# Spare PSUM banks for attention in block 0, later weight splits and loads, and global queries turned without a copy

## The chip, the cores and the metric

The kernel runs on one core of one Trainium2 chip. The metric is device time in microseconds. The kernel before took 1093.67 us, the median of three runs (1090.04 to 1094.86). The profile shown is of one further execution.

## The reference

Sliding-window attention with a few global tokens is followed by a gated MLP, all in f32. Batch 8, 8 heads, 512 local tokens, 32 global tokens, head size 64.

```python
s_g = scale * q_g @ k_all.T          # global queries see all 544 keys
out_g = softmax(s_g) @ v_all
s_ll = where(|i - j| <= 32, scale * q_l @ k_l.T, -1e9)
s_lg = scale * q_l @ k_g.T           # local queries see 65 neighbours and the 32 global keys
out_l = softmax([s_lg, s_ll]) @ [v_g, v_l]
x = [out_g, out_l] as (8 * 544, 512) rows
h = x @ w_in                          # 512 -> 2048
y = (h * sigmoid(h)) @ w_out          # 2048 -> 512
```

## The kernel before, in words

**Tiles and blocks.** The 4352 rows of x are 34 tiles of 128 tokens. A tile of local tokens (batch b, chunk c) is made by four attention steps, one for each pair of heads (pr); k counts the steps, 128 in all. Two further tiles hold the global queries' rows. The MLP takes the tiles in blocks (SIZES, L38): block 0 has one tile, blocks 1 to 11 have three each. A block's MLP has 16 steps f, one for each 128 columns of d_ff: `first_layer(n, f)` (L599) makes h, applies the gate on ACT and DVE, and `second_layer(n, f)` (L628), one step behind, adds to the block's outputs.

**Numbers.** The precision needed is kept in two ways. Early work (attention steps k < 28 for the scores and k < 16 for the rest, batches b < 3 for the global heads, block 0's MLP) is computed in plain f32. Later operands are split into a high and a low part in fp32r, and products are the sum of two or three matmuls. So the weights are wanted in f32 for block 0 and as w_hi and w_lo from block 1 on. They come as 8-byte words: `fetch_weights` (L167) loads a half slice (512 KB) by a DMA that ACT issues, `join_weights` (L175) makes f32 of it with one operation on ACT (L193) and two on DVE (L195, L196), and `split_weights(f)` (L199) makes w_hi on ACT (L206) and w_lo on POOL (L207) for each half of a slice. All of these are pinned behind what was written before them for their engine. The f32 slice 15 lives in the two buffers of klo, which the attention steps from k = 28 on use for the low part of k.

**One attention step.** `st_load`, `st_vload` (DMAs from SP), `st_split`, `st_vsplit`, `st_scores` (PE scores into a bank "s", DVE mask and maximum at L361, ACT exponentials at L365, scaling), `st_turn` (the probabilities are transposed on PE into a bank "t" and copied to pt by ACT, the global columns added by POOL), `st_out` (PE into a bank "o", emptied by ACT and DVE, L459 to L464 or L470 to L471).

**Global heads.** For each batch, `g_load`, `g_split`, `g_scores` (PE into banks "s" and "o", copied to pg by ACT) and `g_soft` run beside the batch before. `g_move` (L266), for b >= 3, copies the 128 x 512 part of pg to an fp32r tile rg with a DMA from SP; rg takes a buffer "o" of the pool `two`, whose two buffers also hold the finished output rows (L645). `g_turn` (L274) transposes four pieces on PE into a bank "o" (gt, L291; from pg in f32 for b < 3, from rg in fp32r for b >= 3), and the last 32 columns into a bank "s" (gu, L294); ACT and DVE copy them out (L292, L297, L298).

**PSUM.** There are eight banks: one each for "s", "t" and "o" (`attbank`, L75), two for h, three for the block's outputs (out0 to out2). Before block 0's MLP begins ("early"), attention also rotates through h and out banks; `early.clear()` ends that. Block 0 has one tile and uses out0 alone.

**The order of the work.** PE executes in the order of the program. The attention steps form a list sorted by due times (`put`, the tables DUE, LATE, HEAD, TURN, MOVE); `fill` (L585) is called after each piece of the MLP and issues from this list so that block n + 1's attention is written out while block n's MLP runs. The other engines' order is made by a scheduler from the program. FIRSTW and FIRSTC say at which early attention steps how many weight halves are fetched and joined; in block 0, step f joins up to slice f + 1 and fetches up to slice f + 3 (LOOK, FETCH). Slice i is split at MLP step SPLIT0 + i, counted from block 0's first step (L663). At a block's last step the program issues from the list until no rg waits for its turn (L642).

Of the kernel before, what the change touches and what calls it, by code (L numbers as in the profile page):

```python
# [9 lines left out]
F32 = mybir.dt.float32  # L10
F32R = mybir.dt.float32r
# [9 lines left out]
P = 128  # L21
# [20 lines left out]
GF = 3  # L42
KP = 12
SCRATCH = 8
FETCH, LOOK = 4, 2
SPLIT0, SPLITS = 11, 1.0
FIRSTW = {1: 2, 2: 1, 3: 1}
FIRSTC = {2: 1, 3: 1}
LATE = dict(load=-1.0, first=0.2, head=0.8, soft=0.3, turn=1.0, slot=4.0)

DUE = dict(load=-1.2, split=-0.5, vload=-0.6, vsplit=0.95, turn=1.6, out=2.2)
LAG = 2.25
HEAD = dict(load=-0.2, split=0.45, scores=0.65, soft=0.85, slot=0.3)
HEADS0, HEADS = (10, 1), (7, 2)
MOVE, TURN = (-0.3, -0.8), (0.7, 1.7)
FULL = 0.98
END = 0.5

# [1 line left out]
def attention_moe_kernel(ctx: ExitStack, tc: tile.TileContext, qk0_in, qk_in, v_in, gqk, wts, out):  # L60
    nc = tc.nc
# [4 lines left out]
    two = ctx.enter_context(tc.tile_pool(name="two", bufs=2))  # L66
# [3 lines left out]
    ps_out = ctx.enter_context(tc.tile_pool(name="ps_out", bufs=1, space=PSUM))  # L70


    early, banks = [1], {"s": itertools.count(), "t": itertools.count(), "o": itertools.count()}

    def attbank(kind, name):  # L75
        if early:
            i = next(banks[kind]) % {"s": 3, "t": 2, "o": 3}[kind]
            if i and kind == "s":
                return ps_h.tile([P, 512], F32, tag="h", name=name)
            if i:  # L80
                return ps_out.tile([P, 512], F32, tag="out2" if kind == "t" else f"out{i - 1}", name=name)
        return ps_att.tile([P, 512], F32, tag=f"att{kind}", name=name)


# [2 lines left out]
    ident = const.tile([P, P], F32R, name="ident")  # L87
# [31 lines left out]
    pgs = [const.tile([P, SKV], F32, name=f"pg{i}") for i in range(2)]  # L119
# [90 lines left out]
    state = {}  # L210
# [39 lines left out]
    def did(what, *needs):  # L250
        for need in needs:
            assert need in order_done, (what, need)
        order_done.add(what)
# [9 lines left out]
        nc.vector.reciprocal(out=st[:, 3:4], in_=st[:, 0:1])  # L263
        nc.vector.tensor_scalar(out=pg, in0=pg, scalar1=st[:, 3:4], scalar2=None, op0=ALU.mult)

    def g_move(b, hh):  # L266
        did(("move", b, hh), ("soft", b, hh))
        if b < GF:
            return
        r0 = two.tile([P, 4 * P], F32R, tag="o", name=f"rg0_{b}_{hh}")  # L270
        nc.sync.dma_start(out=r0.bitcast(F32), in_=pgs[hh][:, : 4 * P])
        state["rg", hh] = r0

    def g_turn(b, hh):  # L274
        whole = b < GF
        if whole:
            r0, idt = pgs[hh], ident.bitcast(F32)
        else:
            r0, idt = state.pop(("rg", hh)), ident
        did(("turn", b, hh), ("turn", b, 0) if hh else ("last", b - 1))  # L280
        if hh == 0:

            state["pgt"] = (work.tile([P, NC, H, SG], F32, tag="pgt", name=f"pgt{b}"),
                            work.tile([P, QG], F32R, tag="pgh", name=f"pgh{b}"),
                            work.tile([P, QG], F32R, tag="pgl", name=f"pgl{b}"))
        pgt, pgh, pgl = state["pgt"]
        hs = slice(4 * hh, 4 * hh + 4)
        tb = attbank("o", f"gt{b}_{hh}")
        for i in range(4):
            sl = slice(i * P, (i + 1) * P)  # L290
            nc.tensor.transpose(tb[:, sl] if whole else tb[:, sl].bitcast(F32R), r0[:, sl], idt)  # L291
        nc.scalar.copy(out=pgt[:, :, hs, :], in_=tb.rearrange("p (t h q) -> p t h q", t=4, h=4))  # L292
        tb = attbank("s", f"gu{b}_{hh}")
        nc.tensor.transpose(tb[:SG, :P], pgs[hh][:, 4 * P :], ident.bitcast(F32))  # L294
        for i in range(2):
            rows, src = slice(SG * (2 * hh + i), SG * (2 * hh + i + 1)), tb[:SG, QG * i : QG * (i + 1)]
            nc.scalar.copy(out=pgh[rows, :], in_=src)  # L297
            nc.vector.tensor_tensor(out=pgl[rows, :], in0=src, in1=pgh[rows, :].bitcast(F32), op=ALU.subtract)  # L298
# [219 lines left out]
    stream, marks = [], {}  # L518
    at = 0.0

    def put(when, fn, *a):
        stream.append((when, fn, a))

    AHEAD = NPR * SIZES[0]
    for k, (t, b, c, pr) in enumerate(steps):
        a = (k, b, c, pr)
        j = k % NST
        lag = LAG if k < AHEAD else 0.0
        if k == AHEAD:
            at += LAG + LATE["first"]  # L530
            for h in range(NPR):
                due = at + LATE["head"] * h
                put(due + LATE["load"], g_load, 0, h)
                put(due, g_scores, 0, h)
                if h % 2:
                    put(due + LATE["soft"], g_soft, 0, h // 2)
                    put(due + LATE["soft"], g_move, 0, h // 2)
                    put(due + LATE["soft"] + LATE["turn"], g_turn, 0, h // 2)
            at += LATE["slot"]
            put(at + DUE["turn"] - 0.1, g_late)  # L540
        if j == 0 and b:
            for hh in range(2):
                put(at + MOVE[hh], g_move, b, hh)
                put(at + TURN[hh], g_turn, b, hh)
        for counts, fn in ((FIRSTW, fetch_weights), (FIRSTC, join_weights)):
            for i in range(counts.get(k, 0)):
                put(at + DUE["load"], fn)
        put(at + DUE["load"], st_load, *a)
        put(at + DUE["split"], st_split, *a)
        put(at, st_scores, *a)  # L550
        put(at + lag + DUE["vload"], st_vload, *a)
        put(at + lag + DUE["vsplit"], st_vsplit, *a)
        put(at + lag + DUE["turn"], st_turn, *a)
        put(at + lag + DUE["out"], st_out, *a, t)
        marks[t] = at + lag + DUE["out"]
        if j == NST - 1 and b % 4 == 3:
            put(marks[t] + 0.001, g_tile, t + 1)
            marks[t + 1] = marks[t] + 0.001
        if b + 1 < B:
            for h in [h for h in range(NPR) if int((HEADS if b else HEADS0)[0] + h * (HEADS if b else HEADS0)[1]) == j]:  # L560
                for part, fn in (("load", g_load), ("split", g_split), ("scores", g_scores)):
                    put(at + HEAD[part], fn, b + 1, h)
                if h % 2:
                    put(at + HEAD["soft"], g_soft, b + 1, h // 2)
                at += HEAD["slot"]
        at += 1.0
    stream.sort(key=lambda e: e[0])
    done = 0

    def advance(to):  # L570
        nonlocal done
        while done < len(stream) and stream[done][0] <= to:
            _, fn, a = stream[done]
            done += 1
            fn(*a)

    ends, t = [], 0
# [50 lines left out]
    def second_layer(n, f, gh, gl):  # L628
        if f == 0:
            outs[n] = [ps_out.tile([P, DM], F32, tag=f"out{i}", name=f"out{n}_{i}") for i in range(SIZES[n])]  # L630
        wh, wl = (w_hi[f][:, DM:], w_lo[f][:, DM:]) if n else (w_32[2 * f + 1], None)
        for i, o in enumerate(outs[n]):
            sl = slice(i * P, (i + 1) * P)
            if n == 0:
                nc.tensor.matmul(o, gh[:, sl], wh, start=(f == 0), stop=(f == NF - 1))
            else:
                nc.tensor.matmul(o, gh[:, sl], wh, start=(f == 0), stop=False)  # L637
                nc.tensor.matmul(o, gh[:, sl], wl, start=False, stop=False)  # L638
                nc.tensor.matmul(o, gl[:, sl], wh, start=False, stop=(f == NF - 1))  # L639
            fill(1)  # L640
        if f == NF - 1:
            while ("rg", 0) in state or ("rg", 1) in state:  # L642
                advance(stream[done][0])
            for i, o in enumerate(outs.pop(n)):
                sb = two.tile([P, DM], F32, tag="o", name=f"o{n}_{i}")  # L645
                nc.scalar.activation(sb, o, AF.Copy, scale=0.5)
                for p0, np_, r in out_rows(sum(SIZES[:n]) + i):
                    nc.sync.dma_start(out=out[r : r + np_, :], in_=sb[p0 : p0 + np_, :])
# [4 lines left out]
    for n in range(len(SIZES)):  # L653
        for f in range(NF):
            if n == 0:
                while w_next[1] < 2 * min(NF, f + LOOK):
                    join_weights()
                while w_next[0] < 2 * min(NF, f + FETCH):
                    fetch_weights()
            elif f == 0:  # L660
                advance(ends[n])
                now[:] = n, 0
            while len(w_hi) < NF and SPLIT0 + SPLITS * len(w_hi) <= NF * n + f:  # L663
                split_weights(len(w_hi))
            g = first_layer(n, f)
            fill(SIZES[n])
            if pend is not None:
                second_layer(*pend)
            pend = (n, f, *g)
# [70 lines left out]
```

## Time and profile before

| | |
|---|---|
| median of three runs | 1093.67 us (1090.04 to 1094.86) |
| the profiled execution | 1088.63 us, span 1086.8 us, granted clock 0.991 |
| PE busy | 1033.7 us, 95% |
| DVE busy | 749.4 us, 69% |
| ACT busy | 734.9 us, 68% |
| POOL busy | 189.6 us, 17% |
| block 0's MLP | from 24 us to 126 us |
| block 1's MLP | from 126 us to 223 us |
| bytes moved by DMA | 128.63 MB |

PE is TensorE, DVE is VectorE, ACT is ScalarE, POOL is GpSimd, SP is SyncE; PEld is the load of weights into TensorE, which overlaps its matmuls. L206 is line 206 of the kernel. Groups of instructions are shown as `line engine operation out<-in shape xcount | busy us, mean ns | idle before <-releaser`; lines in order of time as `start us, length us, engine line operation out<-in`, with the idle time before and its releaser in brackets; waits as `engine line <- what it waited for: us in total, times, longest`. "issue" is waiting for nothing that the profile shows.

### The profile page before, as it was taken

Reading aid. Unit: us, or ns where it says so; the run is one execution under the profiler, and the core shown is the slowest. Engines: PE = TensorE matmul, PEld = TensorE weight load, DVE = VectorE, ACT = ScalarE, POOL = GpSimd, SP = SyncE. Lnnn points to the kernel's source line nnn. Section 1 sums busy time; section 2 is a strip of 40 time slices with the busy share of each in tenths; the row PEclk is TensorE's granted clock in tenths of the full one; section 3 lists DMA queues with packets and bytes.
Section 4 is the critical chain, followed back from the end, with each engine's and each line's share of the span. In section 5 each row is a group of like instructions: output and inputs, shape, how many; then the busy total and the mean of one; then the engine's idle time right before and its main releaser. Section 6 shows DMA issues by size and latency. Waiting matters only on the chain.

```text
span 1086.8 us, 19886 instructions
## 1 busy us (share of the span) xinstructions
PE 1033.7 (95%) x6168; PEld 926.3 (85%) x6168; DVE 749.4 (69%) x2285; ACT 734.9 (68%) x1977; POOL 189.6 (17%) x480
## 2 busy tenths in 40 slices
PE   5786798999999999999999999999999999999997
PEld 4564697899999899999999988998999989999996
DVE  3778574677778777886657877778777877654322
ACT  5676676777778677776657777777777877654322
POOL 2004475211111111111101111111111211110000
PEclk9998999999999999999999999999999999999999
DMA  7885132343344334343224434434433533410000
GB/s 242 283 283 177 63 98 86 113 132 104 111 139 129 122 110 141 124 140 114 72 78 127 155 98 130 123 118 130 140 112 119 161 100 113 127 40 21 30 1 29
DMA packets 68745, 128.63 MB, mean 118 GB/s; under 512 B 7712, under 2 KB 27680, under 8 KB 68640
## 3 DMA queue, kind: packets, MB, share of 16 engines
q1 hardware_dynamic: 64032, 110.59, 32.3%
q10 hardware_dynamic: 4608, 16.78, 4.5%
q8 instruction: 49, 0.80, 0.3%
q14 instruction: 56, 0.46, 0.1%
HBM read 86.44 MB, written 8.91 MB: 88 GB/s over the span
## 4 chain that ended last, share of the span: by engine, by line
PE 87%; DVE 4%; ACT 4%; issue 2%; DMA 1%; POOL 0%; ACTq 0%; DVEq 0%; POOLq 0%
PE h L612 33%; PE out L637 12%; PE out L639 11%; PE out L638 11%; PE s L357 5%; PE o L448 4%; PE o L450 3%; PE t L392 3%; DVE w L196 1%; PE o L444 1%; PE gs L240 1%; ACT probs L365 1%; DMA raw<-in_qk_dram 1%; ACT w_hi L206 1%; PE gt L291 1%
## 5 line engine op out<-in xcount | busy, mean ns | idle before, releaser
L612 PE MATMUL h<-xh,w_hi 128*128 128x384 f32 x704 | 241.4, 343 | 0.0
L612 PE MATMUL h<-xl,w_hi 128*128 128x384 f32 x704 | 238.3, 339 | 0.0
L612 PE MATMUL h<-xh,w_lo 128*128 128x384 f32 x704 | 238.3, 339 | 0.0
L637 PE MATMUL out<-w_hi,gh 128*128 128x512 f32 x528 | 219.6, 416 | 0.0
L639 PE MATMUL out<-w_hi,gl 128*128 128x512 f32 x528 | 208.8, 395 | 0.3 <-DVE gl L625 0.3
L638 PE MATMUL out<-w_lo,gh 128*128 128x512 f32 x528 | 208.1, 394 | 0.0
L618 ACT ACTIVATE t<-h 128x384 f32<-128x384 f32 (+1 forms) x192 | 90.6, 472 | 158.9 <-PE h L612 152.1
L620 DVE SCALAR_TENSOR_TENSOR t<-t,h 128x384 f32<-128x384 f32 x176 | 97.2, 552 | 113.1 <-ACT t L618 111.8
L612 PEld LDWEIGHTS h<-xh,w_hi 128*128 128x128 f32 x704 | 133.0, 189 | 5.1
L612 PEld LDWEIGHTS h<-xl,w_hi 128*128 128x128 f32 x704 | 132.9, 189 | 5.1
L612 PEld LDWEIGHTS h<-xh,w_lo 128*128 128x128 f32 x704 | 132.6, 188 | 0.0
L625 DVE TENSOR_TENSOR gl<-t,gh 128x384 fp32r<-128x384 f32 x176 | 99.2, 563 | 46.1 <-PE out L639 40.4
L365 ACT ACTIVATE probs<-probs,st 128x224 f32<-128x224 f32 x244 | 115.7, 476 | 12.1 <-DVE st L361 10.7
L416 POOL CAST pt_hi<-pgt 128x64 fp32r<-128x64 f32 x112 | 37.7, 336 | 490.1 <-PE o L450 347.7
L639 PEld LDWEIGHTS out<-w_hi,gl 128*128 128x128 f32 x528 | 99.5, 188 | 23.8 <-DVE gl L625 0.7
L361 DVE CUSTOM_DVE_ANT_0 probs<-s,mask 128x224 f32<-128x224 f32 x244 | 85.2, 385 | 43.7 <-PE s L357 42.7
L637 PEld LDWEIGHTS out<-w_hi,gh 128*128 128x128 f32 x528 | 100.0, 189 | 12.4 <-issue 2.0
L638 PEld LDWEIGHTS out<-w_lo,gh 128*128 128x128 f32 x528 | 100.3, 190 | 10.5
L624 ACT CAST gh<-t 128x384 fp32r<-128x384 f32 x176 | 89.8, 510 | 21.5 <-DVE t L620 18.8
L471 DVE TENSOR_TENSOR xs<-o,xs 64x160 f32<-64x160 f32 x224 | 70.7, 315 | 28.5 <-ACT xs L470 24.3
L327 ACT CAST qk<-raw 128x704 fp32r<-128x704 f32 x100 | 78.1, 781 | 16.3 <-PE s L357 14.9
L448 PE MATMUL o<-pt_hi,vv 128*128 128x160 f32 x448 | 87.7, 264 | 0.6 <-DVE xs L471 0.3
(122 smaller groups left out, 1871.8 us busy)
## 6 DMA issues: line engine op xcount, KB each, us to landing
raw<-in_qk_dram SPq DMA_DIRECT2D x100, 352.0 KB, 3.0
rr<-probs SPq DMA_DIRECT2D x112, 256.0 KB, 2.3
raw_w<-in_wts_dram ACTq DMA_DIRECT2D x32, 512.0 KB, 5.7
vraw<-in_v_dram SPq DMA_DIRECT2D x128, 128.0 KB, 2.3
raw_g<-in_gqk_dram SPq DMA_DIRECT2D x32, 304.0 KB, 2.9
out_dram<-o SPq DMA_DIRECT2D x32, 256.0 KB, 2.6
raw<-in_qk_dram SPq DMA_DIRECT2D x28, 240.0 KB, 4.4
rg<-pg SPq DMA_DIRECT2D x10, 256.0 KB, 2.8
```

What stands on the lines that cost most here:

```text
L327: nc.scalar.copy(out=qk, in_=raw)
L361: nc.vector.tensor_tensor_reduce(out=p[:, u, :W], in0=s[:, u * W : (u + 1) * W], in1=mask_of[c], scale=-SCALE, scalar=3.0e38, op0=ALU.add, ...
L365: nc.scalar.activation(p[:, u, :W], p[:, u, :W], AF.Exp, bias=st[:, u : u + 1], scale=-1.0, accum_out=st[:, 2 + u : 3 + u])
L448: nc.tensor.matmul(o[:, at], vv[:, a, u].rearrange("p t d -> p (t d)"), pt_hi[:, u, a, :m], start=(a == 0), stop=(a == 1))
L612: nc.tensor.matmul(h[:, :nt], wt, x[:, c, :nt], start=(i == 0), stop=(i == 3 * NCC - 1))
L618: nc.scalar.activation(t[:, :nt], h[:, :nt], AF.Tanh, scale=0.5)
L620: nc.vector.scalar_tensor_tensor(out=out[:, :nt], in0=t[:, :nt], scalar=1.0, in1=h[:, :nt], op0=ALU.add, op1=ALU.mult)
L624: nc.scalar.copy(out=gh[:, :nt], in_=t[:, :nt])
L625: nc.vector.tensor_tensor(out=gl[:, :nt], in0=t[:, :nt], in1=gh[:, :nt].bitcast(F32), op=ALU.subtract)
L637: nc.tensor.matmul(o, gh[:, sl], wh, start=(f == 0), stop=False)
L638: nc.tensor.matmul(o, gh[:, sl], wl, start=False, stop=False)
L639: nc.tensor.matmul(o, gl[:, sl], wh, start=False, stop=(f == NF - 1))
```

## The change

Four things change.

- In `attbank`, once "early" is over and until block 1's first step, every second tile of the kind "s" takes the bank out1 and every second tile of the kind "o" takes out2 (the list `spare` is cleared at block 1's first step).
- SPLIT0 goes from 11 to 14: slice i is split at MLP step 14 + i, so slices 0 and 1 in block 0 and the other fourteen in block 1.
- FIRSTW goes from {1: 2, 2: 1, 3: 1} to {0: 2, 1: 1, 2: 1, 3: 2}, and these fetches and the two joins of FIRSTC are due just behind the scores of their step rather than with its load, 1.2 units earlier.
- `g_move` is gone, with the loop that waited for rg at a block's end: `g_turn` transposes pg itself, in f32, for all batches.

```diff
-SPLIT0, SPLITS = 11, 1.0
-FIRSTW = {1: 2, 2: 1, 3: 1}
+SPLIT0, SPLITS = 14, 1.0
+FIRSTW = {0: 2, 1: 1, 2: 1, 3: 2}
...
-MOVE, TURN = (-0.3, -0.8), (0.7, 1.7)
+TURN = (0.7, 1.7)
...
-    early, banks = [1], {"s": itertools.count(), "t": itertools.count(), "o": itertools.count()}
+    early, spare, banks = [1], [1], {"s": itertools.count(), "t": itertools.count(), "o": itertools.count()}
...
+        elif spare and kind != "t" and next(banks[kind]) % 2:
+            return ps_out.tile([P, 512], F32, tag="out1" if kind == "s" else "out2", name=name)
         return ps_att.tile([P, 512], F32, tag=f"att{kind}", name=name)
...
-    def g_move(b, hh):
-        did(("move", b, hh), ("soft", b, hh))
-        if b < GF:
-            return
-        r0 = two.tile([P, 4 * P], F32R, tag="o", name=f"rg0_{b}_{hh}")
-        nc.sync.dma_start(out=r0.bitcast(F32), in_=pgs[hh][:, : 4 * P])
-        state["rg", hh] = r0
-
     def g_turn(b, hh):
-        whole = b < GF
-        if whole:
-            r0, idt = pgs[hh], ident.bitcast(F32)
-        else:
-            r0, idt = state.pop(("rg", hh)), ident
-        did(("turn", b, hh), ("turn", b, 0) if hh else ("last", b - 1))
+        did(("turn", b, hh), ("soft", b, hh), ("turn", b, 0) if hh else ("last", b - 1))
...
-            nc.tensor.transpose(tb[:, sl] if whole else tb[:, sl].bitcast(F32R), r0[:, sl], idt)
+            nc.tensor.transpose(tb[:, sl], pgs[hh][:, sl], ident.bitcast(F32))
...
-                    put(due + LATE["soft"], g_move, 0, h // 2)
...
-                put(at + MOVE[hh], g_move, b, hh)
                 put(at + TURN[hh], g_turn, b, hh)
         for counts, fn in ((FIRSTW, fetch_weights), (FIRSTC, join_weights)):
             for i in range(counts.get(k, 0)):
-                put(at + DUE["load"], fn)
+                put(at + 0.01, fn)
...
-            while ("rg", 0) in state or ("rg", 1) in state:
-                advance(stream[done][0])
...
             elif f == 0:
                 advance(ends[n])
+                spare.clear()
                 now[:] = n, 0
```

## The prediction

> **What bounds the kernel now.** I read the page first. Its second part says where TensorE (PE) is not busy; the columns of the rows here are forty equal slices of 27.2 us.
>
> ```profile
> span 1086.8 us, 19886 instructions
> ...
> PE 1033.7 (95%) x6168; PEld 926.3 (85%) x6168; DVE 749.4 (69%) x2285; ACT 734.9 (68%) x1977; POOL 189.6 (17%) x480
> ...
> PE   5786798999999999999999999999999999999997
> ```
>
> PE is idle for 1086.8 - 1033.7 = 53 us, and nearly all of that lies in the first seven slices: the start, block 0 (one tile; weights fetched, joined and first used) and the change to block 1. From there PE is full, so a microsecond saved early is kept to the end, and one saved on another engine later is worth nothing. I cut the early part into stages.
>
> ```profile
> 24.00:126.00 102.00, 75.47 (x423) 54.94 (x422) 74.86 (x252) 69.32 (x195) 22.68 (x38) 0.95 0.65 216
> 41.00:96.00 55.00, 48.42 (x290) 35.88 (x289) 43.96 (x158) 42.08 (x120) 8.18 (x18) 1.00 0.83 275
> 126.00:223.00 97.00, 93.80 (x531) 83.65 (x529) 56.82 (x171) 67.81 (x182) 45.87 (x67) 0.97 0.28 90
> 223.00:312.00 89.00, 88.70 (x549) 80.94 (x548) 69.27 (x214) 66.14 (x182) 15.20 (x44) 1.00 0.38 119
> ```
>
> The columns are stretch, length, then busy time of PE, PEld, DVE, ACT and POOL, granted clock, DMA share, GB/s. Block 0's MLP runs from 24 to 126 us: no engine is above 75 of 102 us, so it is bound by waits in a chain over three engines. Its middle (41 to 96) is already dense, with 55.00 - 48.42 = 6.6 us of PE idle; its two ends, 47 us together, hold 27.1 us of PE work. Block 1 (126 to 223) loses 97.00 - 93.80 = 3.2 us, block 2 nothing. What PE waits for up to 180 us, as total, times, longest:
>
> ```profile
> PE o L444 <- DVE acc L464: 9.5, 3, 7.9
> PE s L357 <- DMA raw<-in_qk_dram: 5.8, 1, 5.8
> PE gt L291 <- DVE acc L464: 4.7, 2, 2.4
> ...
> PE gs L240 <- issue: 3.4, 1, 3.4
> PE gs L240 <- DVE xs L471: 2.9, 1, 2.9
> ...
> PE s L357 <- DVE pgl L298: 1.3, 1, 1.3
> ```
>
> L464, L471 and L298 are the last readers of the single attention banks "o" and "s": these are waits for a PSUM bank to be emptied.
>
> **The spare banks.** While block 0 runs, every second "s" tile goes to out1 and every second "o" tile to out2, which block 0's one-tile output (out0) leaves empty. A PE write then waits for the reader of the tile before last. First case, at 33 us, PE's own order:
>
> ```profile
> 33.01 1.34 PE L240 MATMUL gs<-raw_g 128*64 128x272 f32 x4 [3.40 <-issue]
> 34.28 2.08 PE L635 MATMUL out<-w,gh 128*128 128x512 f32 x2
> ...
> 38.28 1.02 PE L635 MATMUL out<-w,gh 128*128 128x512 f32 x2
> ```
>
> The gs matmuls reuse the "s" bank that gu of the first turn wrote just before, and its readers (L297, L298) are late. With a second bank the 3.40 us go, and so does the slowness behind them: the same two matmuls take 2.08 us after the wait and 1.02 us later, 1.06 us. With the 1.3 us of the second turn: 5.8 us. Second case, at 104 us:
>
> ```profile
> 104.75 2.36 PE L444 MATMUL o<-pt,vraw 128*64 128x160 f32 x8 [7.90 <-DVE acc L464]
> 107.04 1.86 PE L357 MATMUL s<-raw 128*128 128x224 f32 x4
> ```
>
> Third case, the two turns of batch 1 (2.4 us is the longer), with the slowed first layer after them in the chain of waits (start, length, what):
>
> ```profile
> 116.86 0.63 PE L291 MATMUL gt<-ident,pg 128*128 128x128 f32 x4 [2.26 <-DVE acc L464]
> ...
> 120.40 1.30 PE L444 MATMUL o<-pt,vraw 128*64 128x160 f32 x8
> ...
> 126.07 0.67 PE L612 MATMUL h<-xh,w_hi 128*128 128x384 f32 x1
> ```
> ```profile
> 126.42 3.47 PE h L612 x12
> ...
> 206.76 2.11 PE h L612 x12
> ```
>
> The eight L444 matmuls take 2.36 us after the 7.90 and 1.30 at 120 us: 1.1 us of slow clock, 9.0 us with the wait. The turns give 4.7 us and 3.47 - 2.11 = 1.4 us behind them, 6.1 us. The clock is a consequence of the waits here, not a term of its own. [...]
>
> **Slices split from the fourteenth step.** Three of the five slices that were split in block 0 (w_hi on ACT, w_lo on POOL) go to block 1. The 7.90 us have their cause here as much as in the bank: DVE's two join operations from 40 to 89 us, and from 89 to 126 us, when POOL splits.
>
> ```profile
> L196 DVE SCALAR_TENSOR_TENSOR w<-w,raw_w 128x512 uint32<-128x512 uint32 x17 | 11.8, 693 | 0.7 <-ACT w L193 0.4
> L195 DVE TENSOR_SCALAR raw_w<-raw_w 128x512 uint32<-128x512 uint32 x17 | 7.3, 429 | 0.2
> ```
> ```profile
> L196 DVE SCALAR_TENSOR_TENSOR w<-w,raw_w 128x512 uint32<-128x512 uint32 x8 | 8.7, 1088 | 0.4
> ...
> L195 DVE TENSOR_SCALAR raw_w<-raw_w 128x512 uint32<-128x512 uint32 x7 | 5.1, 732 | 0.0
> ```
> ```profile
> L207 POOL TENSOR_TENSOR w_lo<-w,w_hi 128x512 fp32r<-128x512 f32 x10 | 13.9, 1406 | 11.6 <-ACT w_hi L206 10.2 <-DVE pgl L298 1.1 <-POOL pt L410 0.3
> L206 ACT CAST w_hi<-w 128x512 fp32r<-128x512 f32 x10 | 5.7, 615 | 0.0
> ```
>
> DVE loses 8 x (1088 - 693) + 7 x (732 - 429) ns = 5.3 us beside POOL. By the program's order the last join belongs to step 14 and now precedes the first split, so I take all of it back; ACT drops 3/5 of 5.7 = 3.4 us there.
>
> How much of the waits is then really gained? Their sum over the ends of block 0 is 5.8 + 9.0 + 6.1 = 20.9 us, but the other engines need time for what is left. In the two ends DVE has 74.86 - 43.96 - 5.3 = 25.6 us of work. In the dense middle it is 43.96 / 55 = 80% busy; at that share it needs 32 us. ACT: 69.32 - 42.08 - 3.4 = 23.8 us at 42.08 / 55 = 77% gives 31 us. PE: 27.1 less the 1.06 and 1.1 slowed, at 48.42 / 55 = 88%, is 28 us. DVE is late next, and the 47 us become 32: **15 us**, between 9.0 (the late stall alone) and 20.9 plus up to 4 of the middle's 6.6 idle. I take the middle itself at nothing, its waits being short and spread.
>
> **Price in block 1.** Splits now run to its fourteenth step, still one a step, but each slice is needed two steps after it is ordered instead of five. How long one takes, POOL and PE in order of time:
>
> ```profile
> 131.38 2.87 POOL L207 TENSOR_TENSOR w_lo<-w,w_hi 128x512 fp32r<-128x512 f32 x2 [7.33 <-ACT w_hi L206]
> ```
> ```profile
> 137.22 0.50 PE L612 MATMUL h<-xh,w_hi 128*128 128x384 f32 x1
> ```
> ```profile
> 213.17 0.27 PE L357 MATMUL s<-klo,qk 128*128 128x224 f32 x1
> ```
>
> The slice ordered with block 1's first step (126.07 us) is done at 134.25, a lag of 8.2 us; the step two later begins at 137.22, 11.1 us after the order. So there is 3 us of air. The last slice shares its buffers with klo of step 28: ordered with the step that the chain has at 206.76, at that lag its first half (1.4 us before the second) is free near 213.5, while PE wants klo at 213.17 after a DVE subtraction; 0 to 2 us. Block 1's own bank wait (2.9 us) falls among splits, so three slices more than eleven may bring 3/11 of it, 0.8 us. ACT was 67.81 and POOL 45.87 of 97 us busy, room for 3.4 us and 3 x 2 x 1.4 = 8.4 us. I take +2 us, between 0 and 5. DVE's gl, between 126 and 223 and in block 2:
>
> ```profile
> L625 DVE TENSOR_TENSOR gl<-t,gh 128x384 fp32r<-128x384 f32 x15 | 9.5, 631 | 7.9 <-PE out L639 6.6 <-ACT gh L624 1.2
> ```
> ```profile
> L625 DVE TENSOR_TENSOR gl<-t,gh 128x384 fp32r<-128x384 f32 x15 | 8.4, 557 | 1.3 <-PE out L639 1.0
> ```
>
> It pays 74 ns each for POOL's company, 1 us over the block, covered by DVE's 40 us of idle. [...]
>
> **Turns without DMA copies.** Removed: ten copies (g_move), each an issue on SP and one landing, and the two-tile "o" slots they held. Added: forty f32 transposes in place of fp32r ones, straight from pg.
>
> ```profile
> 376.56 0.50 PE L291 MATMUL gt<-ident,rg 128*128 128x128 f32 x4 [1.96 <-issue]
> ```
> ```profile
> PE gt L291 <- issue: 5.2, 7, 2.0
> ```
> ```profile
> L271 SPq DMA_DIRECT2D rg<-pg x10: 470/471/1713, 351.0 to 856.4; - x10
> ```
>
> Four of them take 0.63 us from pg (row at 116.86) and 0.50 from rg: ten turns, **+1.3 us** on a full PE. The 5.2 us of waiting before late turns could be taken for the copies, but the first of these was issued at 351 us and used after 367; a turn follows directly on st_out and needs the same "o" bank, which is unchanged there. So 0, with -5.2 as the bound. SP's 0.47 us per issue was hidden behind PE.
>
> **Weights loaded later.** The first two halves are now issued behind the first softmax on ACT, not at 0.73 us; the fifth and sixth come in the prologue instead of at step 0; the two early joins move behind the scores of their step.
>
> ```profile
> 0.73 0.89 ACTq L172 DMA_DIRECT2D raw_w<-in_wts_dram  x2
> ```
> ```profile
> raw<-in_qk_dram SPq DMA_DIRECT2D x100, 352.0 KB, 3.0
> ```
>
> The first qk tile landed at 5.8 us beside 1 MB of weights; alone, by the larger tile's 3.0 us, it may be there 2 us earlier: between -2 and +2 (ACT, in order, standing before a join whose half has not landed, with the exponentials queued behind it). I take **-1 us**.
>
> **Sum.** -15 + 2 + 1.3 - 1 = -12.7, say -13 us. The profiled execution took 1088.63 us (span 1086.8 and 1.8 around it), which becomes 1076; it is 5 us below the median of the runs, 1093.67, so the same 13 us on the median give **1081 us**.
>
> **The rivals.** (1) *All waits fall*: 20.9 + 4 + 2 gained, 2 paid: -25, 1069 us. For it, the readers named are bank readers in every row; against, DVE's 80%. (2) *Another wait takes their place*: PE runs its order strictly, and pt, which comes through ACT and POOL, is late as often as the bank; or the weight halves become the limit (DMA share 0.83 in the middle). Then the late stall gives 9.0, of which half comes back, and block 1 and the transposes take 3.3: -1 to -2, 1092 us. (3) *Slices too late*, the other side: if the lag in block 1 passes the 11.1 us between order and use, each step costs half the excess. At 14 us that is 14 steps x 1.4 = 20 us, and -13 + 20 = +7, 1101 us. It costs the whole gain from a lag of about 13 us. For it, POOL stands in order behind PE's o matmuls; against, 8.2 us measured.
>
> **How the numbers follow.** Forecast 0.50, rival 1 0.20, rival 2 0.20, rival 3 0.10. The range 1065 to 1096 holds all of the forecast's own (1072 to 1088), rivals 1 and 2, and leaves out rival 3. About 0.5% (5.5 us) is what a measurement of this kernel can tell from no change. Faster by more than that: the forecast but for its thin end, and rival 1, 0.69; within: rival 2 and that end, 0.20; slower: rival 3 and a little of 2, 0.11.
>
> **What would show it.** Right: no PE wait above 3 us between 25 and 126 us; L195 and L196 near 429 and 693 ns throughout; block 1's first step 12 to 18 us earlier; blocks 2 to 11 as long as now but for 0.1 us a turn. Wrong: o or gs waiting for DVE acc still, or for ACT pt in its place; PE's L612 waiting for w_lo in block 1 or for klo at its end; a first qk matmul no earlier than 5.8 us. The forecast falls if block 0 ends where it did, or if block 1 grows by what block 0 sheds.

## The result, and the profile after

The kernel changed takes **1074.27 us**, median of four runs (1073.5 to 1079.43); the kernel before, run beside it, 1092.22 (1090.04 to 1094.86). The ratio is **0.9845, 95% interval 0.9805 to 0.9885**: 18 us faster, where 13 were forecast. The profiled execution took 1074.63 us, 14.0 less than that of before (1088.63).

The page of the changed kernel: span, busy times, PE and its granted clock in forty slices of 26.8 us.

```profile
span 1072.8 us, 19856 instructions
...
PE 1037.6 (97%) x6168; PEld 929.6 (87%) x6168; DVE 748.4 (70%) x2285; ACT 735.1 (69%) x1977; POOL 189.0 (18%) x480
...
PE   6899989999999999999999999999999999999997
PEclk7999999999999999999999999999999999999999
```

PE is idle for 35 us in place of 53, and the low digits of slices 3 to 7 are gone. The last line shows something new: a granted clock of 0.7 in the first slice. Busy time by stage, before and after, in the columns that the prediction used (stretch, length, PE, PEld, DVE, ACT, POOL, granted clock, DMA share, GB/s):

```profile
0.00:24.00 24.00, 13.68 (x73) 10.43 (x73) 8.45 (x37) 12.44 (x34) 5.67 (x22) 1.00 0.73 255
24.00:41.50 17.50, 11.12 (x52) 7.24 (x52) 10.90 (x30) 9.37 (x24) 0.41 (x2) 0.90 0.83 284
41.50:95.80 54.30, 47.72 (x286) 35.18 (x285) 43.76 (x158) 42.08 (x120) 7.98 (x18) 1.00 0.83 276
95.80:126.10 30.30, 16.72 (x91) 12.62 (x89) 20.19 (x65) 17.87 (x51) 14.29 (x19) 0.88 0.21 68
126.00:223.40 97.40, 94.20 (x532) 84.00 (x530) 57.20 (x172) 68.19 (x183) 45.87 (x67) 0.97 0.28 89
```
```profile
0.00:28.40 28.40, 18.55 (x72) 14.27 (x72) 8.63 (x37) 12.84 (x34) 5.68 (x22) 0.76 0.72 252
28.40:42.70 14.30, 10.87 (x53) 7.78 (x52) 10.36 (x29) 9.08 (x24) 0.41 (x2) 0.88 0.77 261
42.70:93.00 50.30, 47.65 (x285) 35.43 (x284) 42.95 (x169) 41.11 (x119) 4.33 (x15) 1.00 0.87 295
93.00:110.40 17.40, 15.30 (x91) 10.92 (x89) 13.99 (x51) 14.43 (x45) 6.91 (x12) 1.00 0.40 132
28.40:110.40 82.00, 73.82 (x425) 54.12 (x423) 67.31 (x247) 64.61 (x187) 11.65 (x29) 0.98 0.76 255
110.40:206.20 95.80, 91.79 (x532) 81.55 (x530) 62.88 (x178) 71.83 (x191) 56.51 (x77) 1.00 0.29 91
```

The stages by these borders, the rest being what remains of the span:

| stage | before | after | difference |
|---|---|---|---|
| start, up to block 0's MLP | 24.0 | 28.4 | +4.4 |
| block 0, first steps | 17.5 | 14.3 | -3.2 |
| block 0, middle | 54.3 | 50.3 | -4.0 |
| block 0, end | 30.3 | 17.4 | -12.9 |
| block 1 | 97.4 | 95.8 | -1.6 |
| the rest | 863.4 | 866.6 | +3.2 |

Block 0 sheds 20 us, most of it at its end; the start and the rest give back 7.6. What PE still waits for in block 0, as total, times, longest:

```profile
PE h L594 <- DVE w L199: 2.9, 3, 1.8
PE gt L281 <- DVE pg L267: 1.7, 1, 1.7
PE o L434 <- ACT pg L248: 1.2, 1, 1.2
```

DVE acc, for which PE waited 14.2 us in the two rows of before, is gone from these rows. h waits for a joined weight, and the turn for the softmax that makes its own operand. Only the third row is still a wait for a bank's reader: L248 is ACT's copy of gs out of its bank. DVE is now busy for 67.31 of 82.0 us, 82%.

### The profile page after: what moved, and what is told of

It reads as the page before. It is cut to its first block, busy times and chain, and to the rows that moved or that the text cites. A ratio compares the mean times of both kernels' runs of the same rounds, so it can differ in the third digit from the quotient of the medians.

```text
span 1072.8 us, 19856 instructions
## 1 busy us (share of the span) xinstructions
PE 1037.6 (97%) x6168; PEld 929.6 (87%) x6168; DVE 748.4 (70%) x2285; ACT 735.1 (69%) x1977; POOL 189.0 (18%) x480
## 4 chain that ended last, share of the span: by engine, by line
PE 85%; ACT 5%; DVE 5%; DMA 2%; issue 2%; POOL 1%; SPq 0%; ACTq 0%; DVEq 0%
PE h L600 33%; PE out L625 11%; PE out L627 10%; PE out L626 10%; PE s L347 5%; PE o L438 4%; PE o L440 3%; PE t L382 3%; DMA raw<-in_qk_dram 1%; PE o L434 1%; PE h L594 1%; ACT probs L355 1%; PE gs L243 1%; ACT w_hi L209 1%; PE gt L281 1%
## 5 line engine op out<-in xcount | busy, mean ns | idle before, releaser
L608 DVE SCALAR_TENSOR_TENSOR t<-t,h 128x384 f32<-128x384 f32 x176 | 97.2, 552 | 108.0 <-ACT t L606 106.7
L612 ACT CAST gh<-t 128x384 fp32r<-128x384 f32 x176 | 89.8, 510 | 23.9 <-DVE t L608 21.2
```

What stands on the lines that cost most here:

```text
L608: nc.vector.scalar_tensor_tensor(out=out[:, :nt], in0=t[:, :nt], scalar=1.0, in1=h[:, :nt], op0=ALU.add, op1=ALU.mult)
L612: nc.scalar.copy(out=gh[:, :nt], in_=t[:, :nt])
```

## The experiments

All ratios are to the kernel before on the same chip. Where an execution is split into stages, the points are block 0's and block 1's first h matmul and block 1's end.

### The change without the spare banks

```diff
-        elif spare and kind != "t" and next(banks[kind]) % 2:
-            return ps_out.tile([P, 512], F32, tag="out1" if kind == "s" else "out2", name=name)
```

> The changed kernel without the spare banks (attention's s and o have one bank each in block 0). Theory A (the bank waits carried most of block 0's 102 us): the waits behind the turns and part of the long one come back, 8 to 14 us on the changed kernel's 1074, so 1082 to 1088, with PE waiting for DVE acc again. Theory B (the slow joins beside POOL's splits carried it, the banks only showed it): 1 to 4 us, 1075 to 1078.

Measured: 1092.39 us (1089.47 to 1096.52), ratio 0.9994 [0.9968, 1.002]. The other three edits together make no difference to the time. In its profile, PE's waits in block 0 and the end of it in order of time:

```profile
PE gt L279 <- DVE acc L452: 5.1, 2, 3.1
PE o L432 <- DVE acc L452: 4.0, 3, 2.4
```
```profile
102.82 1.27 PE L432 MATMUL o<-pt,vraw 128*64 128x160 f32 x8 [2.38 <-DVE acc L452]
...
114.42 0.78 PE L279 MATMUL gt<-ident,pg 128*128 128x128 f32 x4 [3.10 <-DVE acc L452]
```

The 7.90 us wait of before is down to 2.38; by the order of the program, only the later splits of the three edits left in act on this stretch. The turn behind it waited 2.26 us in before and waits 3.10 here, still for the single bank. Block 0 takes 97.2 us (28.65 to 125.84), 4.9 less than before. The trace loses that again elsewhere: block 0 starts 4.65 us later, and what follows block 1 takes 868.0 us in place of 863.4, with 1.9 more in each of blocks 3 and 6. So, as far as these two traces go (1092.54 us and before's 1088.63), the equal medians hide a gain in block 0 and losses outside it. The later splits by themselves, with single banks and early weights, were not run.

### The spare banks alone

The kernel before with the lines above, the list `spare` and its clearing, nothing else.

> The kernel before with the spare banks alone (splits from the eleventh, weights early, copies kept). Theory A (the banks are the whole gain): 15 to 20 us less than before on the same chip, 1073 to 1078 against 1092 to 1095. Theory B (the banks need the later splits beside them, since DVE's joins stay slow): 8 to 12 us less, 1082 to 1087.

Measured: 1077.58 us (1072.33 to 1077.93), ratio **0.9844 [0.981, 0.9879]**, the whole gain. DVE's joins at the end of block 0, from 80 to 126 us, stay slow beside POOL's splits (709 and 435 ns in the changed kernel, 1009 and 640 ns before, in the same stretch):

```profile
L198 DVE SCALAR_TENSOR_TENSOR w<-w,raw_w 128x512 uint32<-128x512 uint32 x10 | 9.0, 903 | 0.4
L197 DVE TENSOR_SCALAR raw_w<-raw_w 128x512 uint32<-128x512 uint32 x10 | 7.6, 761 | 0.1
```
```profile
PE o L446 <- issue: 3.7, 3, 2.7
...
PE gt L293 <- DVE pg L266: 3.1, 1, 3.1
```

The second fence has two of PE's waits of block 0. The 7.90 us are gone here too, with slow joins: the same o matmuls wait 2.7 us, with no releaser named, and acc is left with a single wait of 0.7 us, before a turn. Block 0 takes 88.4 us (23.9 to 112.3).

### One second bank at a time

```diff
-        elif spare and kind != "t" and next(banks[kind]) % 2:
+        elif spare and kind == "o" and next(banks[kind]) % 2:
```

In the other kernel, `kind == "s"`.

> The changed kernel with a second bank for the kind o alone (out2), one for s. By the prediction's rows the waits on s are 3.4 + 1.1 + 1.3 + 1.0 = 6.8 us of the block and those on o the rest: 5 to 7 us more than the changed kernel, 1079 to 1081. Theory B (PE runs in order, so one bank short brings most of the waits back at other places): 10 to 18 us more, 1084 to 1092.

> The changed kernel with a second bank for the kind s alone (out1), one for o. By the rows the waits on o (out after out, gs after out, turns after out) are the larger part: 9 to 13 us more than the changed kernel, 1083 to 1087. Theory B: as for the other bank, nearly all comes back, 1088 to 1092.

Measured: with the o bank 1080.51 us (1077.09 to 1081.14), ratio 0.9884 [0.9838, 0.9929]; with the s bank 1087.26 (1083.14 to 1089.71), 0.9952 [0.9926, 0.9979]. The gains, 1.16% and 0.48%, or 12.7 and 5.2 us of 1092, add up to 1.64%; both banks gave 1.55%. The intervals are 0.3 to 0.5% wide to either side, so the two sizes are rough. PE's waits in block 0, with the o bank doubled, and with the s bank doubled:

```profile
PE s L347 <- issue: 3.0, 2, 1.8
```
```profile
PE gt L281 <- DVE acc L454: 5.4, 2, 3.1
PE o L434 <- DVE acc L454: 4.0, 3, 2.4
```

Each leaves the waits of the bank that stayed single. In the second, gt and o wait behind acc, the last reader of bank o. In the first, s waits with no releaser named; that it waits for bank s is read from its place, as both waits come behind a gu that took the same bank.

### Splits from the eleventh step again

```diff
-SPLIT0, SPLITS = 14, 1.0
+SPLIT0, SPLITS = 11, 1.0
```

> The changed kernel with slices split from the eleventh step again. Theory A (banks): with two banks the joins slowed beside POOL are cushioned, 2 to 5 us more, 1076 to 1079. Theory B (slow joins): 8 to 12 us more, 1082 to 1086. In both the joins L198 and L199 are slow again, 1.5 us each where POOL splits.

Measured: 1074.77 us (1074.02 to 1077.88), ratio 0.9828 [0.9783, 0.9873]: no difference from the changed kernel. The joins of the changed kernel from 80 to 126 us, and of this one:

```profile
L199 DVE SCALAR_TENSOR_TENSOR w<-w,raw_w 128x512 uint32<-128x512 uint32 x10 | 7.1, 709 | 0.0
L198 DVE TENSOR_SCALAR raw_w<-raw_w 128x512 uint32<-128x512 uint32 x10 | 4.4, 435 | 0.1
```
```profile
L199 DVE SCALAR_TENSOR_TENSOR w<-w,raw_w 128x512 uint32<-128x512 uint32 x10 | 9.0, 904 | 0.4
L198 DVE TENSOR_SCALAR raw_w<-raw_w 128x512 uint32<-128x512 uint32 x9 | 7.5, 835 | 0.0
```

So the later splits do to DVE what the prediction said, and beside spare banks the time does not follow. In the trace block 0 is 3.6 us longer here (85.6), the start 2.5 shorter (25.95 us), and what follows block 1 is 1.5 shorter, so the medians have nothing left to show.

### Weights early again, and copies again

The first undoes FIRSTW and `put(at + 0.01, fn)`; the second puts `g_move`, rg and the loop at a block's end back.

```diff
-FIRSTW = {0: 2, 1: 1, 2: 1, 3: 2}
+FIRSTW = {1: 2, 2: 1, 3: 1}
...
-                put(at + 0.01, fn)
+                put(at + DUE["load"], fn)
```

> The changed kernel with the weight halves fetched and joined as before (first two at the start, joins with the load of their step). Theory A (the later loads cost the start: ACT stands before joins whose halves have not landed, and PE's clock falls behind the longer waits): block 0's MLP begins near 24 us instead of 28.5, and the time falls by 3 to 5 us, to 1069 to 1071. Theory B (the later loads help, by the first qk tile at 3.5 us, and the slow clock at the start is chance): no change or 1 to 2 us more, 1074 to 1076.

> The changed kernel with the DMA copies and fp32r transposes of the global queries put back. Theory A (forty f32 transposes cost 0.13 us a turn on a full PE, and nothing waited for the copies): 1 to 2 us less, 1072.5 to 1073.5. Theory B (the copies, their wait on SP or the o buffers, cost something): 1 to 3 us more, 1075 to 1077.

Measured: 1075.3 us (1072.04 to 1078.12), ratio 0.9822 [0.9779, 0.9866], and 1074.56 (1074.17 to 1074.83), 0.9816 [0.9781, 0.9852]. Neither differs from the changed kernel. The first is odd: with the weights early its block 0 began at 28.0 us, not at 24. (The profile is of its longest execution, 1078.12 us.) Two stretches of its start, and the same two of the kernel before:

```profile
14.00:20.00 6.00, 4.50 (x23) 3.60 (x24) 2.32 (x11) 3.54 (x11) 0.00 (x0) 0.66 0.74 274
20.00:26.00 6.00, 5.33 (x19) 3.36 (x17) 0.45 (x2) 1.60 (x4) 0.00 (x0) 0.50 0.00 0
```
```profile
14.00:20.00 6.00, 3.82 (x28) 3.00 (x29) 2.45 (x11) 3.97 (x12) 0.00 (x0) 1.00 0.74 273
20.00:26.00 6.00, 6.00 (x38) 4.18 (x36) 1.60 (x5) 3.66 (x10) 0.00 (x0) 1.00 0.31 85
```

The granted clock is 0.66 and 0.50 where before had 1.00, though PE executes the same groups of matmuls in the same order up to block 0. The DMA is idle in the second stretch. So the clock can fall at the start without the later loads, and the late start there is no matter of weight traffic alone.

### The turns a quarter of a step later

```diff
-TURN = (0.7, 1.7)
+TURN = (0.93, 1.93)
```

> The changed kernel with both turns of a batch 0.23 units later in the order of PE (0.93 and 1.93 instead of 0.7 and 1.7), further behind the out that uses the same bank and ahead of the next. Theory A (the 5.8 us that the turns wait are for the bank o): those waits fall to under 1.5 us, and with the slow clock behind the two long ones the time falls by 3 to 6 us, to 1068 to 1071. Theory B (a turn's own copy then holds up the next out by as much): no change, 1073 to 1075.

Measured: 1098.67 us (1095.49 to 1105.06), ratio 1.0053 [1.0027, 1.0079], 24 us above the changed kernel. Neither expectation was met. PE's waits from 200 us on, in the changed kernel and in this one:

```profile
PE gt L281 <- DVE xs L461: 5.8, 8, 2.0
```
```profile
PE s L347 <- DVE pgl L288: 19.2, 12, 1.9
```

The wait of gt for bank o has gone as intended. In its place the scores (L347) wait twelve times for bank s, whose last reader is the turn's own gu (L288). There are no copies in either kernel: a turn takes both single banks, and its place between two steps decided here which of them was waited for. These rows account for 13.4 us. The profiled execution is this kernel's longest (1105.06 us); against that of the changed kernel, PE is idle 19.5 us more, and the same number of matmuls is busy 11.0 us longer (1048.6 against 1037.6), at a mean clock of 0.981 in place of 0.989.

### PE kept busy through the start's wait

Eleven f32 matmuls of the identity into bank out1, which nobody reads, stand behind the first transposes of the start, where PE waits for ACT:

```diff
+    def keep_busy(n):
+        d = ps_out.tile([P, 512], F32, tag="out1", name=f"busy{n}")
+        for i in range(n):
+            nc.tensor.matmul(d[:, :P], ident.bitcast(F32), ident.bitcast(F32), start=True, stop=True)
+
+    put(3.851, keep_busy, 11)
```

They were put into the changed kernel, into the kernel before, into before with spare banks and SPLIT0 14, and into before with spare banks alone.

> The changed kernel with eleven extra f32 matmuls of the identity by itself (about 2.4 us, result unused, in out1) between the first turn and the first out of the start, where PE waits 3.5 us for ACT. Theory A (that wait lets PE's clock fall to half for some 10 us, from about 15 us on, in most executions): the granted clock stays at 1.00 there, block 0 begins 2 to 4 us earlier, the time is 1069 to 1072 and the executions lie closer together. Theory B (the slow clock at the start comes from elsewhere or by chance): no change, 1073 to 1077, clock again near 0.5 at 15 to 25 us.

> The kernel before with the same eleven matmuls. Its own executions lie between 1088 and 1099 us, the shorter ones at a mean clock of 0.991 and the longer at 0.980. Theory A (the start's clock is what parts them): all near the lower end, 1086 to 1091. Theory B: the same spread and median, 1092 to 1095.

> The kernel before with the spare banks, splits from the fourteenth, and the eleven matmuls; weights early and copies kept as before. Theory A (the later weights and the copies are worth nothing, the clock 2 to 4 us): 1069 to 1072, the same as the changed kernel with the matmuls. Theory B (the later weights gain 2 us by the first tile): 1072 to 1075, slower than it.

> The kernel before with the spare banks and the eleven matmuls at the start, splits from the eleventh: the kernel of the run before it with the later splits undone, which had 1072.15 us (1070.6 to 1073.9) with little scatter. Theory A (with two banks the slow joins still cost a part of their 5.3 us): 2 to 5 us more, 1074 to 1077, block 0 ending later. Theory B (the second bank covers them): 1071 to 1073.

| kernel with the matmuls | us | ratio |
|---|---|---|
| changed kernel | 1073.07 (1068.95 to 1076.57) | 0.9822 [0.9789, 0.9854] |
| before | 1095.17 (1091.19 to 1102.01) | 1.0031 [1.0009, 1.0053] |
| before, spare banks, SPLIT0 14 | 1072.15 (1070.56 to 1073.91) | 0.9824 [0.9796, 0.9851] |
| before, spare banks | 1074.32 (1071.5 to 1076.97) | 0.983 [0.9793, 0.9868] |

The start of the first (from 14 us), of the second, with its block 0 and a turn at the end of that, and of the third with its block 0:

```profile
14.00:20.00 6.00, 4.16 (x24) 3.29 (x24) 3.12 (x7) 3.13 (x8) 0.00 (x0) 0.82 1.02 406
20.00:26.00 6.00, 5.27 (x21) 3.34 (x20) 0.28 (x1) 2.14 (x5) 0.00 (x0) 0.61 0.31 110
```
```profile
14.00:20.00 6.00, 3.86 (x29) 2.89 (x28) 2.41 (x11) 3.96 (x12) 0.00 (x0) 1.00 0.74 271
...
24.00:130.00 106.00, 78.45 (x423) 57.31 (x422) 74.75 (x252) 69.66 (x195) 23.30 (x38) 0.92 0.63 208
...
118.29 0.63 PE L291 MATMUL gt<-ident,pg 128*128 128x128 f32 x4 [3.66 <-DVE acc L464]
```
```profile
14.00:20.00 6.00, 3.72 (x28) 2.83 (x28) 2.47 (x11) 4.03 (x12) 0.00 (x0) 1.00 0.75 282
...
24.10:105.80 81.70, 72.18 (x424) 52.79 (x423) 66.98 (x247) 64.88 (x187) 11.53 (x29) 1.00 0.79 268
```

In the changed kernel the matmuls fill one wait and the clock falls all the same, a little later. In the kernel before, the start runs at full clock, and block 0 is nonetheless 106 us long at 0.92; the time does not improve. So this long execution (1095.23 us) is not long by its start: its turn waits 3.66 us for bank o's reader where before waited 2.26.

The last two rows of the table differ by SPLIT0 alone. Beside spare banks the later splits are worth about 2 us by the medians, 0.7 by the ratios to before on each kernel's own chip, and the intervals part neither from nothing. The traces show where it goes: with SPLIT0 14 block 0 takes 81.7 us in place of 87.4, block 1 97.7 in place of 97.0, and the rest 866.8 in place of 863.3, of which blocks 3 and 6 lose 1.5 and 1.6. The third kernel has the shortest start and block 0 of all, 105.8 us to block 1 against 110.4, and its ratio still can't be told from the changed kernel's (0.9845).

## Why the prediction was right, and where its terms were off

The sign and the place held: the waits for the banks "s" and "o" in block 0 were the bound, and a second bank removes them. 1074.27 lies within the forecast's own 1072 to 1088. Of the signs it named, block 1's first step came 15.7 us earlier (12 to 18 were forecast), and no PE wait in block 0 is above 1.8 us. That blocks 2 to 11 stay as long as they were did not hold for block 3, which is 1.9 us longer.

The size is in part luck. Between the profiled executions -14.0 us stand against -12.7 of the sum, but stage by stage the terms were off by more, and the errors cancel: the start came out 5.4 us worse than forecast and the later blocks 1.9, the middle of block 0 4.0 us better, block 1 3.6 and the ends of block 0 1.1.

**The spare banks (forecast -15).** Right in mechanism, and nearly in size: the two ends of block 0 went from 47.8 us to 14.3 + 17.4 = 31.7, where the step that put DVE at 80% gave 32. Two parts of the term were off. The middle was taken at nothing, with up to 4 us as its bound, and gave 4.0; its PE idle time fell from 54.30 - 47.72 = 6.6 us to 50.30 - 47.65 = 2.7. Its waits were "short and spread", but two of them, 1.4 and 1.7 us, were for acc as well.

The term also mixed two edits. "The 7.90 us have their cause here as much as in the bank" is true of the wait: with the later splits and single banks it is 2.38, with the spare banks and early splits 2.7. Of the time it isn't shown: the banks alone bring the whole gain (0.9844), the other edits without them nothing (0.9994), and with the banks the later splits have no worth that the runs can tell from none, though block 0 itself gets shorter by them. One bank at a time, 12.7 us belong to o and 5.2 to s. Sorted by bank, the prediction's cases are 9.0 + 6.1 = 15.1 us for o and 5.8 for s, the same order and nearly the same sizes.

**Splits (DVE gets 5.3 us back, block 1 pays +2).** The first half was right, 709 and 435 ns where 1088 and 732 stood. Of the price only a part shows. Block 1 of the changed kernel, POOL, DVE and PE in order of time:

```profile
120.91 3.02 POOL L210 TENSOR_TENSOR w_lo<-w,w_hi 128x512 fp32r<-128x512 f32 x2
...
192.21 1.70 DVE L318 TENSOR_TENSOR klo<-raw,qk 128x448 fp32r<-128x448 f32 x1 [1.56 <-POOL w_lo L210]
...
195.12 0.26 PE L440 MATMUL o<-pt_lo,vv 128*64 128x160 f32 x1 [0.70 <-DVE pt_lo L404]
```

A slice ordered at 115.45 was done at 123.93 (120.91 + 3.02), a lag of 8.5 us where 8.2 were taken, and PE never waited for w_lo: rival 3 fell. klo of step 28 did wait for the last slice, 1.56 us, as the bound of 0 to 2 had it; DVE makes pt_lo two instructions later, and PE waits 0.70 for it. In all PE's idle time in block 1 rose from 3.2 to 95.80 - 91.79 = 4.0 us. The block is 1.6 us shorter all the same, because two slowed stretches of before are missing (clock 1.00 in place of 0.97): the first layer, the 1.4 us counted with the banks, and the matmuls behind the 2.86 us wait of gs. Behind the same wait, 3.54 us pass in before from that gs to the next h, and 2.07 here. That second one was no part of the forecast. DVE's gl paid for POOL's company,

```profile
L613 DVE TENSOR_TENSOR gl<-t,gh 128x384 fp32r<-128x384 f32 x15 | 10.7, 713 | 3.6 <-PE out L627 2.1 <-ACT gh L612 1.5
```

713 ns against 631, beside DVE's 33 us of idle in the block: covered, as forecast. What POOL's 8.4 moved us cost DVE shows in the length of its instructions here, 15 x 82 ns = 1.2 us for gl, and not in the time.

**Turns (+1.3).** Blocks 2, 4, 6, 7 and 9 are each 0.2 to 0.4 us longer, about 1.5 together, as forecast. With the copies put back, blocks 4, 7 and 9 are as long as before to within 0.1 us, and the time of the whole kernel doesn't differ. That the 5.2 us of waits are for the bank and not for the copies was right: they are 5.8 now, without copies, and the profile names the bank's reader.

**Weights later (-1).** The runs don't bear this step out. The first score matmul is 2.3 us earlier, but what follows loses more than that, PE and ACT in order of time:

```profile
3.50 5.84 PE L347 MATMUL s<-raw 128*128 128x224 f32 x16 [3.50 <-DMA raw<-in_qk_dram]
...
14.11 1.97 PE L434 MATMUL o<-pt,vraw 128*64 128x128 f32 x8 [3.52 <-ACT pt L387]
15.79 0.70 ACT L196 ACTIVATE w<-raw_w 128x512 f32<-128x512 f32 x1 [0.97 <-DMA raw_w<-in_wts_dram]
```
```profile
14.79 1.09 PE L444 MATMUL o<-pt,vraw 128*64 128x128 f32 x8 [3.09 <-ACT pt L397]
```

The same eight matmuls take 1.97 us where before (second fence) they take 1.09, and ACT stands before a join whose half has not landed, as the upper bound had it. Block 0 begins 4.4 us later, beyond the bound of +2. The eight kernels with late weights began block 0 at 25.1 us or later, the six with early weights at about 24 but for one at 28.0. So late weights may favour the slow start, but it comes without them too. The weights put back made no measurable difference to the time, so the edit's worth stays at nothing within about 0.4%, and why the clock falls at the start in some kernels and not in others stays open.

**From the profile to the median.** -14.0 between the two profiled executions stands against -18 between medians. The profiled execution of before was among its shortest: its executions in these runs go from 1087.73 to 1099.65 us, at mean granted clocks of 0.991 to 0.978. Taking the same difference for both was the main step that made 1081 too high; that the long ones are long by bank waits which the spare banks also remove is likely, but was not shown for them. One trace speaks for it, of before with the eleven matmuls at 1095.23 us: its block 0 is 3.9 us longer, and behind the turn's wait of 3.66 us in place of 2.26 it takes 6.9 us from the h to the second layer in place of 4.2.

## What to carry to other kernels

Where one engine runs strictly in program order and waits for the readers of single PSUM banks, look for banks that lie empty in that stage. Run each part of a change alone: a part that visibly does its work (faster joins, fewer DMAs, an earlier load) may show nothing in the time, as here, where the later splits took 5.7 us off block 0 in one pair of traces and the later blocks gave 4.2 back. Before a turn or a similar step is moved, list every single buffer that it takes: moving it away from one may move it onto another.

## What the runs showed of the chip that was not expected

**Short waits can halve the pace behind them.** In blocks 3 and 6 of the changed kernel, PE in order of time:

```profile
359.83 0.67 PE L281 MATMUL gt<-ident,pg 128*128 128x128 f32 x4 [2.01 <-DVE xs L461]
...
360.84 0.52 PE L600 MATMUL h<-xl,w_hi 128*128 128x384 f32 x1
361.16 0.52 PE L600 MATMUL h<-xh,w_lo 128*128 128x384 f32 x1
...
363.88 0.34 PE L600 MATMUL h<-xh,w_lo 128*128 128x384 f32 x1
...
623.75 0.63 PE L281 MATMUL gt<-ident,pg 128*128 128x128 f32 x4 [2.01 <-DVE xs L461]
...
624.50 0.33 PE L600 MATMUL h<-xl,w_hi 128*128 128x384 f32 x1
```

Behind a wait of 2.01 us the matmuls start 0.32 us apart in place of 0.17, for about 3 us, at a granted clock of 0.55 (360.6 to 364 us), which costs 1.5 us; this makes up most of block 3's +1.9. In block 6 the same turn waits the same 2.01 us (last two lines), and the h behind it are 0.17 apart, at a clock of 1.00 (624.5 to 628 us): nothing is slowed. In the kernel before, the turn of block 3 waited 1.96 us, and nothing was slowed either. The two waits of 2.01 us in one execution rule out any bound on the single wait's length alone. What else decides it the runs do not show.

**The same order of work starts in two ways.** Block 0 begins at about 24 us with the clock at 1.00, or at 25 to 30; in the eight late profiles that were split at these points the clock was 0.50 to 0.82 from 14 to 20 us, and in all but two of them 0.50 to 0.77 in the next 6 us. Filling one wait with matmuls did not mend it. What decides it stays open.
